# Two more row blocks transposed by DMA, and a new written-out order, in a four-layer attention kernel

## The chip, the core and the metric

The kernel runs on one core of a Trainium2 chip. The core has a matrix engine (TensorE, "PE" in the profile; its weight loads are shown apart as "PEld"), a vector engine (VectorE, "DVE"), an activation engine (ScalarE, "ACT"), a general engine (GpSimd, "POOL") and a queue engine that here only starts transfers (SyncE, "SP"). Each works through its own list of instructions in order; between lists there are only semaphores. The metric is the device time of one execution in microseconds (us). Three executions before the change took 422.68, 423.28 and 421.19 us; their median is 422.68.

## What is computed

The input is 2048 rows of 512 numbers. Four layers follow each other: linear attention (A), attention in a sliding window (B), A again and B again, the weights of A and of B being the same both times.

```python
def _A_ref(x, wqkv, wo):            # 32 heads of 16
    qkv = (x @ wqkv) ...
    phi = lambda t: jnp.where(t > 0, t + 1, jnp.exp(t)) + 1e-6
    pq, pk = phi(q), phi(k)
    kv = jnp.einsum("bhsd,bhse->bhde", pk, v)
    z = jnp.einsum("bhsd->bhd", pk)
    num = jnp.einsum("bhqd,bhde->bhqe", pq, kv)
    den = jnp.einsum("bhqd,bhd->bhq", pq, z)[..., None] + 1e-6
    return (num / den) ... @ wo

def _B_ref(x, wqkv, wo):            # 32 heads of 16, window of 256
    scores = jnp.einsum("bhqd,bhkd->bhqk", q, k) * (Dh ** -0.5)
    mask = (idx[:, None] - idx[None, :] >= 0) & (idx[:, None] - idx[None, :] < W)
    p = _softmax(jnp.where(mask, scores, -1e9))
    return jnp.einsum("bhqk,bhkd->bhqd", p, v) ... @ wo

x = x + _A_ref(_layernorm(x), A_wqkv, A_wo)
x = x + _B_ref(_layernorm(x), B_wqkv, B_wo)
x = x + _A_ref(_layernorm(x), A_wqkv, A_wo)
x = x + _B_ref(_layernorm(x), B_wqkv, B_wo)
```

A sum over all rows (`kv`, `z`) stands in the middle of each A layer: no row of it can be finished before the keys and values of every row are known. A B layer needs only the rows of its window.

## The kernel before

The rows are cut into 16 blocks of 128. All of x stays on the core (tiles `xres`, one for each block).

One block goes through a layer like this. DVE takes the statistics of its rows (lines 814, 815 and 817), POOL the inverse root (818), and DVE writes the normalised block `xn` (820). The matmuls need it transposed: `transp` (from line 823) does that either by a DMA transpose that SP starts (line 828), or by four PE transposes into PSUM (line 835) and a copy out of PSUM (line 845), which ACT or DVE can do. Which block goes which way is listed in `BYPE`. The transposed block is `xTa` in A layers, `xT` in B layers, and `oT` after attention, before the output projection.

PE then projects: keys, values and outputs with four 512-wide matmuls (line 858, two instructions of the plan for a projection), queries of A and queries and keys of B with sixteen 128-wide ones (line 870). In A layers, ACT and DVE compute phi (lines 879 to 885), PE adds keys times values up over the blocks (916), DVE masks the sum (1220), and PE and DVE make the outputs (942 to 954). In B layers, ACT or DVE copy the projections out of PSUM (keys at line 971, twice with a mask each; queries and values at 845), POOL starts DMAs that spread the values (981), PE makes scores (1007 for the two outer half pieces of the window, 1056 for the inner four pieces, 1063 for a mask in the last block), ACT takes their exponentials (1035, 1077), DVE masks them (1043, 1095), PE multiplies with the values (1113, 1125; 1158 and 1167 in the last block), DVE divides (1135, 1137), and the output projection is added to x (893 for A, 894 for B). The last block of the last layer is cut finer, so that the end is short (`b_end`, lines 1148 to 1213).

Keys and values of the third layer, with their sum in `kvacc` (1316), are interleaved with the attention of the second. So the run has these stages: keys and values of layer one; outputs of layer one and start of layer two; attention of layer two with keys and values of layer three behind it; the sum over all rows; outputs of layer three and start of layer four; attention of layer four; the end.

Nothing on the core decides the order. All the work is recorded as about 2,760 operations, and `ORDER` (line 328) is one long text that names them by number in the order in which they are to be laid out:

```python
for word in self.plan.split():
    word, _, at = word.partition(":")
    o = self.ops[int(word.rstrip("'"))]
    o.eng, cost = list(o.engs.items())[word.endswith("'")]
```

A number is an operation, the digits after a colon are the buffers or PSUM banks that its results take, and an apostrophe says that a copy goes to the second engine that can do it (DVE in place of ACT). Each engine's list is the sequence of its own operations in that text. Semaphore waits are then put in where an operation needs what another engine makes, or a buffer that another still uses. So the text sets the order on each engine, the split of the copies between ACT and DVE, and the use of the banks. The costs in the code (0.38 us for a group of transposes, and so on) only serve the laying out of such a text; the chip doesn't see them.

In the first layer, `BYPE` sends blocks one to six (numbers 0 to 5) through PE and the other ten through SP's DMA transposes. SP's list starts with the loads of x, between them one weight, and has the first layer's transposes next, the loads of the other weights (lines 775) behind them, and then the transposes of the later layers.

Of the kernel before, what the change touches and what calls it, by code (L numbers as in the profile page):

```python
# [334 lines left out]
230:5.0 194 299 231 184 224:4.0.0 200' 148 207:9 214:7.1 215 300 238:0 271:10 196 195 197 216 208:2.1.3 209 210 180 225 228 284 212 179 278:7.2 279 272:6.2.1  # L335
152 285 286:1 181 301 302:2 314 315 316 169 211 280' 255:11 226 227 229 273 317 213 318:3 256:3.3.2 257 274 239:12 232' 275 25 16 258 259 34 260 23 261 24
262:4.3 263 26 27 246:7.4 240:2.4.0 185 241 247 276 264' 287:13 244 288:5.5.3 201 289 303:14 290 291 310:6.5 311 312' 292 242 248 319:15 294:3.6 277 304:4.7.2
305 308 295 320:5.6.1 306 321 322 324 217 326:2.7 327 243 28 29 17 245 233 249 265 293 307 309 296' 281 297 313 323 328 325 329 330:0 331:1 378:7.4.0 379 380
# [9 lines left out]
658' 671 626 627 672 673 902:6 907:2 684 903 986:0.4.1 987 988 919 449:0 904 955 905:3 881:1 906:3 882:3 883 921:0.6.0 922 923 908 909 685 686:2 687:1 450:5  # L348
884 1407 960:3.0.3 451 961 910:2 911 677:2.1.5 678 912:2 989 962 1408 924 1409 452 474:6.0 475 476 488 477 478:2 479:3 937:3 938 679 933:0.4.1 934 935 674:2.1
675 700 701 1410 932 939 940:1 720 964:0.6.2 702 703 965 966 688:5.0 689 690 691 1411:3 936 942:4 1412:0 941:1 489:0.3 490 943 501 676' 1021:2.6.2 1022 944  # L350
1023 704:0 491 492 493:0 494:1 705:3 967 692:5.2 693 945:2 946 947:0 680 963 721 694' 956:0.2.0 957 958 954 480:4 481 482 644 645 662 1418:7.1 995:0.5.4 996
997 722:1 723:2 1419 1420' 990 913:4 914 915 968:0.2.5 969 970 495:7 496 713:6.2.0 714 715 959 503 497 504:0.0 505 999:4.2.1 1000 1001 972:7 971 977:6 506 973
507 508:3 1056:0.4.0 1057 1058 1024 736 737 974 975:1 738 976:2 978 979 991:0.2.0 992 980:3 981 1421 1422 1423 998 710:7.3 711 712' 993 706:6.1 707 708' 709'
1030:0.4.3 681 716 1031 1032 695:3.1.1 696 994 948:2 1002 1003:0.6.2 697' 1004 949 950 1435 509:3 982:2 510:5 983:4 984 1005 1006 663 1034:0.2.5 1035 985 1036
511 1012:7 512 772 1436 1437 739 1438 740:2 741:4 1060 1007:6 1008 1439:3 1440:2 1424 1449 1450 1091:0.4.1 1092 754 1093 513:3.12.1 514 515 1013 1014 1009
1010:2 1451 517 1011:0 1026:0.4.0 1027 1028 728:2.0 1015:0 1016 1413:3.1.0 1414 1415 729 755 1425:0 1426:1 698 1037 1065:0.6.1 1066 730' 1416 1417 1067
731:5.0.3 732 724:4.2 733 725 1038:0.2.2 1039 1040 1441:7.0.2 1446:6.0 1447 1442 1029 1025 1033 1042:5 1443 1069:0.2.4 1070 1071 726' 1095 1043 727'
1427:4.4.3 1428 1429 699 1452 1448' 1453:1 1041 1047:6 1044 1126:0.2.2 1127 756 1444 1445 1068 746:7.1 747 1017:1 1045:1 1454:5 1046:1 1128 1430 1431 1048
1094 1061:0.4.0 1062 1063 1049 748' 1050:3 1051 757 1052:0 758:2 759:0 1018:3 1019 1100:0.6.3 1101 1102 1020 1465 1466 1467 1460:2.4 773 774 1455:5.3.0 1456
1073:0.3.5 1103 1461 1074 1457 1462 1432:7.3 742:6.3 1433 743 1075 775 1072 1059 1064 1077:2 1078 744 1458 1459 1104:0.4.2 1105 1106 1076 1434' 1079 1082:3  # L360
1083 745' 1080:2 1081:3 516 717 1161:0.6.0 1162 1163 1084 1085:0 764:2.2 765 1086 518 1087:2 766' 1096:0.4.0 1097 1098 1130 749:3.1.2 750 767:2.2.4 776:3 1107
1165 1135:0.6.1 1136 751' 1137 768 769' 1053:5 777:3 1054 1108:0.3.4 1099 1055 1479 760:2.4 761 762' 1468 1109 1110 1111 734 1112:7 1139:0.5.5 1140 1141 1113
1114 763' 1115:1 770 1469:0 1117:4 1118 1116:2 752 1196:0.2.1 519:5.3 1129 520 1197 521 522 1198 523:0 524:3 1119 1120:2 543:7.13.2 544 545 1480 1121 547
1088:1 1199 1131:2.5.0 1142 1089 1090 782:4.3 783 1164 1493 1132 1133 1134 528:7.14.3 1138 1170:0.2.3 1171 784' 1172 529 530 532 778:6.5 779 780' 781' 525:5
526 1143:0.2.2 753 1144 1145 527 790 791 735 1147:4 1148 792 1122:1 1494 1149 1150:0 1146 1151:1 1174:0.6.4 1175 793 1176 794:1 546 1470:3 1476:5.2 1477
1471:3.2.0 1478' 1177 1472 1473 1474 1475 1152:4 1153 1231:0.6.2 1232 1233 1481 531 1482 1154 1155:1 1156 1123:5 533 1124 1166:0.2.0 1125 1507 1173 558:4.15.1
# [3 lines left out]
1484:4 1269 1504:4.6 1505 1204 812:0 1240:0.6.3 1241 1242 1158:2 1159 1502 1506' 1503 1510 1160 1523 1192:3 1524 1193:3 1194 1195 1537 807 1213:0.4.4 1214  # L370
813:2 1217:2 1215 1218 1219 1220:1 1221:2 1244:0.6.5 1245 1246 1485:3.7.1 549:4.3 1212 550 551 1538 552 553:3 554:1 1539 1216 1486 1487 1488 1489 818:2.1 819
820 814:1.1 1235 1236:4.6.0 1237 815 816' 1243 1238 821:0.2.0 822 823 1247 1239 1463:5.4 817 1275:2.6.1 1464 1222:0 1223 1224 1276 1277 1248:2.4.2 1249 1525
# [996 lines left out]
```

## Time and profile before

| | |
|---|---|
| median of 3 executions | 422.68 us (421.19 to 423.28) |
| the profiled execution | 422.47 us |
| its span, first to last instruction | 421.1 us |
| granted TensorE clock in the span | 1.000 |
| busy: PE, DVE, ACT, POOL | 392.3, 382.3, 383.6, 106.0 us |
| instructions of PE | 8330 matmuls, 8404 weight loads |
| DMA transposes | 115 (25 for xTa, 30 for xT, 60 for oT) |
| program loaded by queue q8 | 68 packets, 1.11 MB |

The profile is of one execution. "Busy" is the time in which an engine had at least one instruction in work, so overlapping instructions count once, while the duration of one instruction counts its whole way through the engine: two equal instructions that follow each other can start closer together than one takes. A matmul is two instructions, a weight load (PEld) and the matmul itself (PE). "Idle before" and "waited for" name who ended an idle time of an engine. "issue" stands where the profile shows no such cause. The chain of waits is found by going back from the last instruction, at each step to what released it.

### The profile page before, as it was taken

The page shows a single profiled execution, that of the slowest core. Times are in us where ns is not written, and L with a number is a line of the kernel's source. Part 1 is how long each engine was busy: PE and PEld are TensorE (multiplying, and loading weights), DVE is VectorE, ACT ScalarE, POOL GpSimd, SP SyncE. Part 2 cuts the span into 40 slices and gives each one's busy share as a digit, 9 for nine tenths or more (in the row PEclk, how much of TensorE's full clock was granted, in tenths as well). Part 3 has the DMA queues.
Part 4 walks back from the last instruction along what each step waited for, and adds up shares of the span by engine and source line. Part 5 has one row for each costly group of instructions (what it writes and reads, how often), then busy time and mean ns, then how long its engine had stood idle before and what let it go on. Part 6 is the DMA issues. An engine that isn't in the chain of part 4 may idle for free.

```text
span 421.1 us, 18887 instructions
## 1 busy us (share of the span) xinstructions
PE 392.3 (93%) x8330; PEld 284.2 (67%) x8404; DVE 382.3 (91%) x1003; ACT 383.6 (91%) x496; POOL 106.0 (25%) x202
## 2 busy tenths in 40 slices
PE   7999989999999899998999999998999899988997
PEld 3655766776766676767586667676767667666675
DVE  7999899999999899998999899999999999978774
ACT  4888679999999999999899767899999999999995
POOL 2230024225232231423131100332322212605200
PEclk9999999999999999999999999999999999999999
DMA  8334426314252130523141201324415422406143
GB/s 265 112 64 138 128 55 126 66 41 99 41 68 43 38 67 16 85 41 59 39 80 22 48 9 39 70 48 68 79 34 80 60 52 33 90 16 117 43 103 92
DMA packets 75720, 29.22 MB, mean 69 GB/s; under 512 B 65264, under 2 KB 73584, under 8 KB 75632
## 3 DMA queue, kind: packets, MB, share of 16 engines
q1 hardware_dynamic: 70336, 22.36, 26.4%
q0 software_dynamic: 4096, 4.46, 5.7%
q8 instruction: 68, 1.11, 1.1%
q10 hardware_dynamic: 1200, 1.11, 0.9%
q14 instruction: 20, 0.16, 0.1%
HBM read 6.29 MB, written 2.10 MB: 20 GB/s over the span
## 4 chain that ended last, share of the span: by engine, by line
PE 42%; ACT 33%; DVE 18%; issue 3%; DMA 3%; POOL 0%; DVEq 0%
ACT pF L1077 23%; PE ps L858 16%; PE ps L870 8%; ACT pH L1035 6%; PE ps L1125 6%; PE ps L1056 5%; PE ps L1113 3%; DVE stats L814 2%; DVE o L954 2%; ACT kbd L971 2%; DMA w_Av<-in_A_wqkv_dram 2%; DVE pF L1095 1%; DVE xres L893 1%; PE ps L916 1%; PE ps L1007 1%
## 5 line engine op out<-in xcount | busy, mean ns | idle before, releaser
L1077 ACT ACTIVATE pF<-ps 128x1024 bf16<-128x1024 f32 x240 | 229.4, 1085 | 4.4 <-PE ps L1056 2.6
L818 POOL TENSOR_TENSOR rstd<-mv,const 128x1 f32<-128x1 f32 x64 | 39.1, 617 | 241.6 <-DVE mv L817 238.6
L981 POOL DMA_DIRECT2D vbd<-vt x128 | 67.1, 532 | 48.2 <-DVE vt L845 30.6
L1035 ACT ACTIVATE pH<-ps 128x1024 bf16<-128x1024 f32 (+1 forms) x64 | 60.3, 1022 | 3.5 <-PE ps L1007 3.2
L1125 PE MATMUL ps<-vbd,pF 128*128 128x34 bf16 x1856 | 60.2, 178 | 2.4 <-issue 2.4
L1125 PEld LDWEIGHTS ps<-vbd,pF 128*128 128x128 bf16 x1856 | 53.3, 96 | 5.5 <-issue 2.7
L1056 PE MATMUL ps<-qT,kbd 32*128 32x128 bf16 x1920 | 48.5, 216 | 5.0 <-ACT pF L1077 2.1
L1095 DVE TENSOR_TENSOR pF<-pF,const 128x512 bf16<-128x512 bf16 (+2 forms) x116 | 46.6, 415 | 3.6 <-ACT pF L1077 3.5
L879 ACT ACTIVATE E<-ps 128x512 bf16<-128x512 f32 x64 | 40.1, 630 | 9.8 <-PE ps L870 6.4
L814 DVE BATCH_NORM_STATS2 stats<-xres 128x6 f32<-128x512 bf16 x64 | 44.0, 689 | 2.0 <-DMA xres<-in_A_x_dram 1.1
L1056 PEld LDWEIGHTS ps<-qT,kbd 32*128 32x128 bf16 x1920 | 28.5, 92 | 22.6 <-ACT pF L1077 9.6
L1043 DVE TENSOR_TENSOR pH<-pH,const 128x1024 bf16<-128x1024 bf16 (+1 forms) x64 | 41.1, 649 | 0.0
L870 PE MATMUL ps<-xT,w_Bq 128*128 128x128 bf16 x512 | 35.5, 219 | 1.0 <-ACT pF L1077 0.7
L870 PE MATMUL ps<-xT,w_Bk 128*128 128x128 bf16 x512 | 35.6, 219 | 0.6 <-ACT pF L1077 0.4
L1113 PEld LDWEIGHTS ps<-vbd,pH 128*128 128x128 bf16 x928 | 29.0, 96 | 8.3 <-issue 2.2
L870 PE MATMUL ps<-xTa,w_Aq 128*128 128x128 bf16 x512 | 34.2, 219 | 0.3 <-DVE pq L883 0.2
L858 PE MATMUL ps<-w_Ak,xTa 128*128 128x512 bf16 (+2 forms) x121 | 32.3, 372 | 1.6 <-issue 0.8
L858 PE MATMUL ps<-w_Av,xTa 128*128 128x512 bf16 (+1 forms) x128 | 32.7, 371 | 1.1 <-issue 0.5
L1113 PE MATMUL ps<-vbd,pH 128*128 128x34 bf16 x928 | 32.7, 178 | 0.9 <-DVE kbd L971 0.3
L858 PE MATMUL ps<-w_Ao,oT 128*128 128x512 bf16 (+2 forms) x119 | 29.4, 354 | 4.2 <-issue 1.6
L870 PEld LDWEIGHTS ps<-xT,w_Bk 128*128 128x128 bf16 x512 | 29.8, 98 | 5.0 <-issue 0.9
L870 PEld LDWEIGHTS ps<-xT,w_Bq 128*128 128x128 bf16 x512 | 29.5, 98 | 5.3 <-issue 2.0
(96 smaller groups left out, 625.6 us busy)
## 6 DMA issues: line engine op xcount, KB each, us to landing
vbd<-vt POOLq DMA_DIRECT2D x128, 34.0 KB, 2.4
xres<-in_A_x_dram SPq DMA_DIRECT2D x16, 128.0 KB, 5.7
out_dram<-xres SPq DMA_DIRECT2D x15, 128.0 KB, 2.3
oT<-o SPq DMA_TRANSPOSE x60, 2.8
w_Ak<-in_A_wqkv_dram ACTq DMA_DIRECT2D x1, 512.0 KB, 5.4
w_Av<-in_A_wqkv_dram ACTq DMA_DIRECT2D x1, 512.0 KB, 6.9
w_Aq<-in_A_wqkv_dram SPq DMA_DIRECT2D x1, 512.0 KB, 7.0
w_Ao<-in_A_wo_dram SPq DMA_DIRECT2D x1, 512.0 KB, 3.9
```

The lines of the kernel that those rows point to most:

```text
L814: s.op(n + ".st", {"DVE": 0.595}, lambda e, en: e.bn_stats(a_st, x.h[:]), reads=[x], writes=[st])
L858: i = e.matmul(g.h[:, a:b], xT.h[:, kt, :], w.h[:, kt, a:b], start=(kt == 0), stop=(kt == 3), skip_group_check=True)
L870: i = e.matmul(g.h[:, f * P:(f + 1) * P], w.h[:, kt, f * P:(f + 1) * P], xT.h[:, kt, :], start=(f == 0 and kt == 0), stop=(kt == 3), skip_ ...
L879: s.op(n + ".e", {"ACT": _act_cost(512)}, lambda e, en: e.activation(E.h[:], g.h, ACT.Exp, bias=0.0), reads=[g], writes=[E])
L981: return [e.dma_start(vbd.h[64 * a:64 * a + 64, j, a], vt.h[64 * j:64 * j + 64, a]) for j in range(2)]
L1035: return e.activation(d, c, ACT.Exp, bias=0.0, scale=DH ** -0.5)
L1043: return e.tensor_tensor(v, v, tr, ALU.mult)
L1056: i = e.matmul(ss[r // 2].h[:, r % 2, k * P:k * P + P], kbds[fj[m] // 2].h[32 * r:32 * r + 32, f, fj[m] % 2, :], qT.h[32 * r:32 * r + 32, ...
L1077: s.op("e%d%d" % (u, g), {"ACT": _act_cost(1024)}, lambda e, en, S=ss[g], pb=pb, g=g: e.activation(pb.h[:, 2 * g:2 * g + 2, :], S.h, ACT.E ...
L1095: return e.tensor_tensor(v, v, tr, ALU.mult)
L1113: i = e.matmul(U.h[:, c:c + 34], pH.h[:, 4 * r + f, 64 * a:64 * a + P], vbds[j // 2].h[:, j % 2, :, 4 * f + r, :], start=first[0], stop=Tr ...
L1125: i = e.matmul(U.h[:, c:c + 34], pFs[at[f, m][0]].h[:, r, at[f, m][1] * P:at[f, m][1] * P + P], vbds[fj[m] // 2].h[:, fj[m] % 2, :, 4 * f ...
```

## The change

`BYPE` is changed so that blocks five and six of the first layer (numbers 4 and 5) are no longer in it. Their transposes become DMA transposes that SP starts, and their two copies out of PSUM are no longer recorded, so there are two operations fewer and later numbers shift by two. The whole text of `ORDER` is replaced. The description of the change says that it was laid out with a late rule for instruction fetches. The rule itself is not in the code, only the order that came of it.

```diff
 ORDER = """
-37 4 0 3 6 7 1 8 9 2 68 61:7 69 70 5 67 71 72:0 73:6.0 62 38 66 85 86 87 10 39 40 88 41 42 43 44 45 46 11 33 12 13 20 47 89:1 22 74 75:7.0.0 76 90:6.1 81:5.0
...
+4 2 37 38 66 6 0 61:7 1 7 8 9 41 68 42 43 44 45 69 70 46 5 3 71 72:0 73:6.0 47 62 67 39 40 74 85 86 87 88 10 75:7.0.0 76 11 12 89:1 33 25 90:6.1 91 13 102
...
 """
-BYPE = {("x1.", t) for t in range(6)} | {("a2.", 15), ("k2.", 15), ("o3.", 0), ("x3.", 0), ("a3.", 15)} | {("o2.",0),("x2.",0)}
+BYPE = {("x1.", t) for t in range(4)} | {("a2.", 15), ("k2.", 15), ("o3.", 0), ("x3.", 0), ("a3.", 15)} | {("o2.",0),("x2.",0)}
```

What the new text does to the lists of the engines:

- PE: two groups of four transposes fewer. The rest are the same operations in another sequence, with the same stages block by block.
- SP: eleven loads of x in a row, then twelve transposes of the first layer, then the weights. Before, ten loads, two transposes, a load, and eight transposes stood there. The blocks' sequence was 6, 7, 9, 8, 12, 11, 10, 13, 14, 15 by number and is now 4, 5, 7, 6, 9, 8, 11, 13, 14, 10, 12, 15.
- ACT and DVE: of the copies that either can do, 24 full ones that DVE did go to ACT and 20 that ACT did go to DVE, and one small copy of the last block goes to ACT. Two copies of ACT, those behind the PE transposes, are gone.
- The end: the score matmuls of the last block's last piece stand ahead of, no longer behind, four matmuls of an output projection of another block and some of the last block's own matmuls with values.
- Buffers and PSUM banks are assigned anew throughout. The text ends a line earlier, so lines behind it have numbers that are lower by one in the new kernel.

More of the change, by code (lines that the diff above doesn't have):

```diff
@@ L348 @@
[L348 to L359, printed above, removed]
@@ new lines @@
+1019:0.6.2 1020 1021 501 944 690:3.2 691 987 478:2 954:0.4.0 955 956 692' 953 1022 479 678 1416:3.1 1417 716 993:0.6.4 1418' 911:5 912 965 994 995 480 913
+1419 966:0.3.5 703:3 967 711:2.2.0 502:6.1 945:1 660 661 957 503 504 505 493:5 494 495 968 969 712 713 997:0.3.1 998 999 506:2 970:5 975:2 971 1054:0.6.0 717
+718 719 734 735 972 976 977 1055 1056 752 753 989:0.3.0 679 990 973:2 974:3 978:3 979 1000 704:5.1 988 705 706' 707' 736 708:2.3 737 996 709 710' 714 991 992
+1028:0.6.3 1029 1030 1420 1421 720:1 507:3 508:4 1422 693:5.1.1 694 695' 1001:0.2.2 1002 1003 509 510 946:7 947 948 1032:0.5.5 1033 1005:4 1006 1004 1423:2
@@ new lines @@
+1134 1135 516 1085:1 1051:6 1097 1052 1053 765:7.2.4 1477 1106:0.4.2 1107 1108 766 767' 768 758:6.4 759 760' 761' 1137:0.2.5 1138 1139 775:3 1110:7 1111 1109
+517:4.2 518 519 520 1112 1113:3 1114:3 1115:6 521:0 1194:0.2.1 1195 1196 1086:7 1087 541:5.13.2 542 545 543 1116 1129:0.2.0 1130 1127 1131 1163 1088 750 751
+1136 1491 776:7.5 777 1128 778' 526:5.14.3 527 530 1117 779' 1168:0.2.3 522:2 780:7.3 1118:0 1119 1120:0 528 1132 529 531 781 782' 1478 1479 1480 523:6 524
+525 788 1492 789 790 1140 1169 1170 1141:0.4.1 1145:7 1142 1146 1143 1144 1147 1148:1 791 792:1 1149:1 1493 1172:0.2.2 1474:6.7 1469:5.7.0 1475 1173 1476'
@@ new lines @@
+793:1 1174 1175 1470 1471 1472 1150:4 769 1229:0.2.2 1230 1231 1121:7 1122 1473 1151 1494 1495:2 1496:4 1481:3 1482:7 1164:0.5.0 1123 1152 1505 1153:3 1154
+1171 1165 1166 1167 783:3.0.5 784 532:0.2 794:2.0 1155:3 533 534 535 536:2 1198 1506 1507 1203:4.6.4 785 801:3.1.1 802 803' 1204 1205 1206 795 796 797' 1180:5
+1176:0.6.5 1508 1181 1177 556:4.15.1 557 1178 558 1233 1179 1197 560 798:3.0 799 800' 1207:0.6.1 1208 1209 1182 1183:0 1184:0 1185:4 1186 1264:0.2.0 1265 1266
+1187 544 546 1188:1 1189 537:1 538:7 539 540 806 1199:0.5.0 1200 1201 807 808 1156:4 1157 1497:7.3.3 1158 1498 1499 1238:0.2.3 1239 1240 1690:6.16.0 1691
@@ new lines @@
+2326:0 2327:1 2318 2354 2347:0.4.2 1807:7 1808 1809 2025:6.2.4 2348 2349 65 2342 2374:0.2.1 2026 2322 2027' 2375 2298:7 2376 2299 2300 2066 2067 2387:0.4.5
+2328:6 1831:2.1 1832 1833 1834 2388 2389 2350 1835:3 1836:1 2068 2035:0 2028 2018:7.5 2019 2329 2330 2331:3 2020 2021 2390 2332 2346 2379:0.4.3 2380 2381 2377
+1822:3 2022:2.3 1823 2355:0.6.0 2356 1824 2084 2085 2023 2024' 2382 2359:5 2360 2357 2358 2383:0.3.4 2384 2361 2362:2 1837:2 1838 2229 2069 2070:1 2086 2385
+2363:2 2378 2029 1839 2102 2410:0.6.2 2411 2412 2262:5 2333:0 2036:4.0 2263 2264 2423:0.2.2 2424 2425 2037 2038 2386 1846:6.0 1847 1848 1849 2364:5 2087
@@ new lines @@
+2566 2590:5.0.1 2591 2592 2557 2541 2542:0 2115:3.2.4 2116 2337 2543:1 2547:1 2548 2571:4.6.4 2572 2573 2117' 2558 2126:2.5 2127 2128' 2129' 2595:0.4.5 2596
+2597 2574 2594 2570 2575:3 2576 2577 2578:3 2599:6.0.2 2579:0 2600 2478:2 2479 2480 2151:5.0.1 2626:3.6.2 2601 2627 2628 2513:1 2152 2153' 2602 2144:2.0 2145
+2598 2146' 2147' 2593 2606 2549:0 2639:0.3.0 2640 2580:5 2581 2582 2583:2 2584 2641 2642 2607:6.0.1 2608 2148:2.2 2149 2118 2119 2611:3 2631:6.4.4 2612 2150'
+2629 2442:2 2613 2614:0 2609 2615:3 2632 2610 2633 2161:1 2635:0.6.5 2636 2634 2637 2443 2444 2445 2514:5 2154 2155 2515 2516 2585:3 2662:0.3.0 2663 2664
```

87 lines of the change are left out of this document (33 added, 54 removed), and 82 rows, old and new, of the table ORDER.

## Prediction

> **What bounds the kernel now.** I began with the page.
>
> ```profile
> span 421.1 us, 18887 instructions
> PE 392.3 (93%) x8330; PEld 284.2 (67%) x8404; DVE 382.3 (91%) x1003; ACT 383.6 (91%) x496; POOL 106.0 (25%) x202
> PE 42%; ACT 33%; DVE 18%; issue 3%; DMA 3%; POOL 0%; DVEq 0%
> ```
>
> Three engines are busy nine tenths of the time and the chain of work that ended last passes through all three, so no single engine is the bound. The busy times were therefore read stage by stage (columns: stretch, its length, then the busy time of PE, PEld, DVE, ACT and POOL, clock, DMA share, GB/s).
>
> ```profile
> 0.00:44.60 44.60, 42.12 (x293) 23.09 (x298) 37.97 (x133) 34.09 (x60) 10.01 (x26) 1.00 0.53 158
> ...
> 110.00:160.00 50.00, 46.47 (x1099) 34.18 (x1100) 46.93 (x109) 47.49 (x58) 11.80 (x22) 1.00 0.28 47
> 160.00:200.00 40.00, 37.65 (x872) 27.70 (x882) 37.15 (x99) 39.12 (x49) 12.08 (x20) 1.00 0.32 53
> 200.00:252.00 52.00, 50.40 (x977) 35.91 (x985) 48.21 (x124) 44.05 (x61) 9.30 (x17) 1.00 0.22 40
> 252.00:281.00 29.00, 26.52 (x469) 20.41 (x472) 28.26 (x78) 24.84 (x40) 5.96 (x11) 1.00 0.28 54
> 281.00:405.00 124.00, 114.88 (x3008) 86.44 (x3029) 112.22 (x272) 122.87 (x139) 36.46 (x69) 1.00 0.36 62
> 405.00:421.10 16.10, 13.72 (x383) 10.18 (x385) 9.16 (x25) 11.42 (x16) 0.00 (x0) 1.00 0.38 94
> ```
>
> The first stage (keys and values of the first layer) belongs to PE: 42.12 of 44.60 us, most of the rest before its first weights land. From 160 to 200 ACT is idle for 0.88 us in 40, from 200 to 252 PE for 1.6 in 52, from 252 to 281 DVE for 0.7 in 29, and from 281 to 405 ACT for 1.1 in 124. An edit is worth something only on the engine that its stage belongs to.
>
> Next, what the chain of waits shows as time in which nothing visible was waited for, and PE's own list of waits.
>
> ```profile
> 117.92 0.60 issue
> 140.42 0.77 issue
> 151.20 0.68 issue
> 288.11 0.31 issue
> ```
>
> ```profile
> PE ps L1125 <- issue: 2.4, 4, 0.8
> ACT pF L1077 <- PE ps L1063: 0.7, 1, 0.7
> ```
>
> The four pieces are the first line of the waits: 2.4 us in four stops, each in the middle of a run of equal matmuls (probabilities times values, line 1125), where a wait for another engine makes no sense. Two stretches cut at the first three stops, and the DMA of the 2.4 us ahead of the second one, say what they are.
>
> ```profile
> 118.20:140.80 22.60, 21.14 (x500) 15.38 (x505) 21.29 (x54) 21.99 (x29) 6.52 (x13) 1.00 0.35 56
> 140.80:151.50 10.70, 9.77 (x252) 7.31 (x252) 9.64 (x22) 10.04 (x12) 4.07 (x8) 1.00 0.24 53
> ```
>
> ```profile
> q8 instruction: 1, 0.02, 3.7%
> ```
>
> Between stops lie 505 and 252 weight loads, each with its matmul: 1010 and 504 instructions, with the few semaphore instructions that are not counted 4 x 256 and 2 x 256. PE takes its program in pieces of 256 instructions, and each stop is such a piece arriving late. That is the "instruction fetch" of the change's title. The fetch does a second thing, which another piece of the chain and the DMA under it show:
>
> ```profile
> 56.26 4.38 DMA xT<-xn
> ```
>
> ```profile
> q8 instruction: 1, 0.02, 2.0%
> ```
>
> A DMA transpose with a fetch under way took 4.38 us; the transposes of the first stage usually took 2.5 (below). So the "late rule" can mean either: pieces of the program that come late, or transposes that land late beside a fetch. What the change says in code is only the new order.
>
> **Part 1: two row blocks to DMA.** Removed are two groups of four PE transposes and two copies by ACT (line 845).
>
> ```profile
> 18.13 0.39 PE L835 MATMUL ps<-const,xn 128*128 128x128 bf16 x4
> ```
>
> ```profile
> 16.30 0.86 PE ps L858 x4
> 17.16 0.89 PE ps L870 x16
> 18.06 0.24 PE ps L916 x4
> 18.30 0.22 PE ps L835 x4
> ```
>
> ```profile
> L845 ACT ACTIVATE xTa<-ps 128x512 bf16<-128x512 bf16 x7 | 4.5, 637 | 6.0 <-PE ps L835 5.9
> ```
>
> The timeline of PE (first row: start, length, line) gives block six's group 0.39 us, the chain (the next four rows: start, its share, line) 0.22, since it begins before the matmuls ahead of it end. I take 0.35, nearer the row that has the whole group: two groups give 0.7 us (0.4 to 0.8), and they count in full, since the stage is PE's. The two copies (1.3 us at 637 ns) leave an engine that is idle for 10.5 us of the stage: nothing.
>
> Added are two DMA transposes on SP's queue. Their cover:
>
> ```profile
> 14.00 0.40 DVE L820 TENSOR_SCALAR xn<-xres,mv,rstd 128x512 bf16<-128x512 bf16 x1
> ```
>
> ```profile
> 4.55 5.75 SPq L775 DMA_DIRECT2D xres<-in_A_x_dram  x10
> ...
> 21.08 16.17 SPq L828 DMA_TRANSPOSE xTa<-xn  x8
> ```
>
> ```profile
> DMA to landing us min/median/max: 2.4/2.5/2.5
> ```
>
> ```profile
> DMA to landing us min/median/max: 2.4/2.5/5.1
> ```
>
> (The two landing rows are those of tile xTa up to 45 us and over the whole run.) The normalised block five is ready at 14.4 in the old order; in the new one its place on DVE's list is earlier. SP has issued its loads by 10.3, and the eleventh, which now stands ahead too, adds some 0.6 us, so SP waits for DVE and not the other way. Landing takes 2.5 us, or 5.1 at worst, so the block is there between 16.9 and 19.5. When PE needs it follows from the chain rows: at 16.30 in the old order PE had done all that the new one puts ahead of block five's first key matmul, but for one key and one value projection (0.86 each), one query projection (0.89) and one 0.24, while block five's transpose (0.35) falls away: 16.30 + 2.85 - 0.35 = 18.8. The block is covered by 1.9 us, or costs 0.7 at worst; I take nothing. Block six is needed two projections and a 0.24 later, and I take its cover to be the same. Behind the transposes in SP's queue stand the weights of the later stages. Eight issues with their waits took 16.17 us; twelve from 14.4 would, even at that rate, end at 38.7 instead of 37.3, and the stage that uses these weights begins after 44.6. Nothing moves there.
>
> **Part 2: the new order.** Every engine's list is rearranged, but block by block the sequence of stages is the same. Three differences can be priced.
>
> The stops. From start to start of the rows below come the paces: 0.34 us for 16 scores of line 1056, 0.41 for 16 of lines 1125 and 1113, 0.35 for 32 of line 1007; the chain rows above give 0.22 for one of line 858 and 0.89 for 16 of line 870. With these I added up the PE work in each piece of 256 instructions:
>
> ```profile
> 138.24 0.40 PE L1056 MATMUL ps<-qT,kbd 32*128 32x128 bf16 x16
> 138.58 0.57 PE L1125 MATMUL ps<-vbd,pF 128*128 128x34 bf16 x16
> 138.99 0.56 PE L1113 MATMUL ps<-vbd,pH 128*128 128x34 bf16 x16
> ...
> 139.88 0.41 PE L1007 MATMUL ps<-qT,kbd 32*128 32x64 bf16 x32
> 140.23 0.19 PE L1125 MATMUL ps<-vbd,pF 128*128 128x34 bf16 x1
> ```
>
> The pieces ahead of the stops at 117.92, 140.42 and 151.20 hold 3.6, 2.7 and 2.9 us of work in the old order; in the new order the pieces at the same three counts hold 4.8, 4.2 and 4.2, and the shortest piece anywhere holds 3.3 instead of 2.7. Short pieces are consumed before the next has come, so I expect these three stops to go. The piece ahead of 288.11 holds 4.7 us in the old order and 4.9 in the new: there shortness was not the cause, and its 0.3 may stay. The worth of all this lies between nothing (ACT, idle 2.5 us from 110 to 160, would be the next late one, or pieces of 3.3 stop in their place) and 2.4 us. I take 1.4, two thirds of the first three stops' 2.05, nearer the upper end because the chain runs through each of them.
>
> The Trainium skill, Runtime: NRT & Kernel Launch, section "Instruction fetch mechanics", speaks against this gain: the sequencer fetches the next block of 256 instructions while it executes the current one, and the cost of crossing a boundary is mostly hidden. The trace agrees on the 256 and not on the cost, with its 2.4 us in four stops. By the page the gain of 1.4 would be nothing.
>
> The end. In the old order ACT's last two exponentials waited 0.7 us for the score matmuls (the second waits row above), and ahead of these stood, among others, an output projection of another block:
>
> ```profile
> 411.90 1.30 PE ps L858 x6
> ```
>
> In the new order four of these six, and three groups of values matmuls, stand elsewhere: the scores come over 0.86 us earlier. The ACT wait of 0.7 bounds the gain above; nothing is the lower bound, as the values matmuls now follow later. I take 0.6.
>
> The copies out of PSUM. By the lists, 24 full copies went from DVE to ACT and 20 the other way: four more for ACT, beside one small one at the end. Counted by place on ACT's list: four more between the scores of blocks twelve and sixteen of layer two (about 163 to 226 us), one fewer up to the next layer's scores, one more net behind them.
>
> ```profile
> 95.67 1.15 ACT kbd L971 x2
> ...
> 269.98 1.32 DVE kbd L971 x2
> ```
>
> One costs ACT 0.575 and saves DVE 0.66. Three fall where ACT has 8 us of idle time in 52: covered, and 1.7 us if that cover is gone. One falls where ACT has 0.88 in 40, one in the stage that belongs to ACT: 1.15 us at most, nothing at least. I take 0.8, a loss. What DVE saves, 2.6 us, comes ahead of the stage of 252 to 281 that is DVE's, in one that is PE's: I take nothing, and 2.6 as the bound.
>
> Sum: -0.7 - 1.4 - 0.6 + 0.8 = -1.9. The profiled execution took 422.47 us with 1.4 around its span; 422.47 - 1.9 = **420.6**. The median of the three runs, 422.68, is 0.2 above the profiled one. What I can't read from lists is whether 2,760 rearranged operations bring small waits of their own.
>
> **The rivals.** *The fetch costs nothing.* ACT, at 47.49 of 50 us, is late next when PE's stops go, or other pieces stop. For it speaks ACT's share, against it that the chain stays on PE through all three stops. Time: 422.47 - 0.7 - 0.6 + 0.8 = 422.0. This is also how it would go by the page's sentence.
>
> *The copies hit ACT.* If the new order closes the idle time that ACT has from 200 to 252, all four copies delay the exponentials behind them, 2.3 us. It decides once less than 2.3 of those 8 us is left on ACT, and then PE's stops and the end gain nothing, as ACT would have been late anyway: 422.47 - 0.7 + 2.3 = 424.1, slower than before. For it speaks that ACT is full on both sides of the stage; against it that PE, with 1.6 us idle in 52, is what ACT waits for there.
>
> *DVE's relief arrives.* If the shorter DVE list lets the third layer start early, its 2.6 us come on top: 418.0. Against it: PE had no room ahead of that barrier.
>
> **How the numbers follow.** Forecast 0.44, fetch costs nothing 0.27, copies hit ACT 0.18, DVE's relief 0.11. About 0.5%, 2.1 us, is what a measurement of this kernel can tell from no change, so "faster" begins at 420.6: half of the forecast, the last rival and a little of the rest, 0.40. "Slower" begins at 424.8, beyond the second rival's own time; a third of that rival with new waits added, and a tenth of what is left, give 0.15. The rest, 0.45, is no change. The forecast's own range, from its bounds, is -0.7 - 2.4 - 0.7 = 418.7 to 422.5; with the other cases 417.8 to 424.2.
>
> **What would show it.** After: no "issue" wait at line 1125, or one under 0.8 us in total; line 835 on xn with 28 matmuls and the first stage's last key-value matmul some 0.7 us before 44.6; no wait of PE for xTa's DMA at 19 to 22 us; no ACT wait for line 1063 at the end; ACT busy about 1 us longer and DVE 2 to 3 us shorter. Wrong would be: stops of the same total elsewhere, PE waiting for a transpose in the first 25 us, or an ACT that is idle more than 37.5 us in all.

## The result, and the profile after

| | before | after |
|---|---|---|
| median, the two kernels run in turn | 421.75 us (421.06 to 423.28) | 419.05 us (418.38 to 419.54) |
| ratio, 95% interval | 1 | 0.9929 [0.9913, 0.9944] |
| the profiled execution | 422.47 us | 418.38 us |
| its span | 421.1 us | 417.1 us |

The change makes the kernel 0.7% faster: 2.7 us by these medians, 3.0 by the ratio of 0.9929; the prediction was 1.9 us. The two profiles lie 4.1 us apart because that of before is 0.7 us above its median and that of after is the fastest of six. Of any difference between these two traces some 1.4 us is therefore the choice of the execution.

The head of the page after, with the busy times, the chain's shares by engine, and a group that had stops before (its last two columns: mean ns of one, idle time ahead of it):

```profile
span 417.1 us, 18964 instructions
PE 401.3 (96%) x8402; PEld 283.5 (68%) x8402; DVE 379.2 (91%) x998; ACT 383.3 (92%) x499; POOL 106.7 (26%) x202
ACT 47%; PE 41%; DVE 10%; issue 1%; DVEq 0%
L1124 PE MATMUL ps<-vbd,pF 128*128 128x34 bf16 x1856 | 59.6, 178 | 0.0
```

Lines of code behind the text are one lower than before, so line 1124 is the old 1125. The 2.4 us that it waited for nothing visible are zero. "Issue" has gone from 3% to 1% of the chain, some 8 us, but the stops are only 2.4 of them. PE's busy time can't be compared as it stands, since the trace of before has 74 matmul records fewer than weight loads, all of them at line 858; that of after lacks none. Where such a record is missing the profile shows PE idle, mostly for 0.16 us, although it worked, and about 3.5 us of the fall of "issue" stand at this line. ACT is as busy as before (383.3 for 383.6 us), DVE 3.1 us less. Line 834 on xn now has 28 matmuls for 36, and no wait of PE for an xTa made by DMA is in the list of the first 45 us.

The stages after, cut at the same events as before where a stage got shorter (stretch, length, busy PE, PEld, DVE, ACT, POOL):

```profile
0.00:43.55 43.55, 41.89 (x289) 22.44 (x290) 38.30 (x135) 31.73 (x58) 10.94 (x26) 1.00 0.58 169
...
110.00:160.00 50.00, 48.85 (x1136) 34.84 (x1138) 47.73 (x119) 48.59 (x60) 16.04 (x30) 1.00 0.28 51
160.00:200.00 40.00, 39.57 (x877) 28.28 (x877) 36.97 (x96) 39.63 (x52) 8.25 (x16) 1.00 0.34 58
200.00:249.10 49.10, 48.48 (x955) 34.36 (x953) 43.68 (x115) 42.72 (x60) 9.72 (x17) 1.00 0.19 37
```

From 110 to 249 us PE is now idle for 2.2 us in 139.1; the same stretches of before had 7.5 in 142. Most of this fall is not the chip's. The same two stretches for line 858 alone (line 857 after; busy PE, PEld) show it:

```profile
110.00:252.00 142.00, 53.78 (x231) 21.41 (x258) 1.00 0.27 46
```

```profile
110.00:249.10 139.10, 58.22 (x258) 21.36 (x256) 1.00 0.26 48
```

For as many weight loads before has 27 matmul records fewer and 4.4 us less busy time. PE's real idle time before was therefore some 3.1 us, 2.05 of them the three stops. The first stage is a microsecond shorter.

Where the time went is read best from the start of the same operation in each trace. "Stage one" is the first masked sum of layer one (line 1220, DVE); "block 12" the first exponential of block 12 in layer two; "sum" the first masked sum of layer three; "block 16" the first exponential of the last block in layer four; "last" the last operation of DVE (line 1213). All in us, from the traces.

| trace | stage one | block 12 | sum | block 16 | last | span |
|---|---|---|---|---|---|---|
| before | 44.60 | 163.57 | 252.19 | 403.90 | 419.54 | 421.1 |
| after | 43.55 | 160.46 | 249.11 | 400.07 | 415.31 | 417.1 |
| difference | -1.05 | -3.11 | -3.08 | -3.83 | -4.23 | -4.0 |

So 1.05 us come from the first stage, 2.06 from the stretch that held three of the four stops, nothing from there to the sum (the stretch of the copies), 0.75 from there to block 16 of layer four, and 0.4 from the end. These are two executions. With nothing changed in it, the first stage ends between 44.25 and 44.60 us in three traces of the old order, and at 43.55 and 43.80 in two of the new one.

The 0.75 us are not the fourth stop, which lay in that stretch: two traces of the old order without it (experiment 1 with +66, and experiment 2) took 151.8 us for the stretch, before took 151.7, and after took 151.0. ACT, which the prediction gave this stage to, has less to do there (busy PE, PEld, DVE, ACT, POOL; before, then after):

```profile
252.19:403.90 151.71, 140.43 (x3453) 106.11 (x3480) 139.56 (x344) 146.42 (x176) 42.42 (x80) 1.00 0.35 61
```

```profile
249.11:400.07 150.96, 144.38 (x3480) 106.20 (x3478) 138.97 (x344) 145.43 (x175) 43.19 (x80) 1.00 0.35 62
```

No run takes this part of the new order alone.

### The profile page after: what moved, and what is told of

Read it like the earlier page. It is cut to its first block, busy times and chain, and to the rows that moved or that the text cites. A ratio compares the mean times of both kernels' runs of the same rounds, so it can differ in the third digit from the quotient of the medians.

```text
span 417.1 us, 18964 instructions
## 1 busy us (share of the span) xinstructions
PE 401.3 (96%) x8402; PEld 283.5 (68%) x8402; DVE 379.2 (91%) x998; ACT 383.3 (92%) x499; POOL 106.7 (26%) x202
## 4 chain that ended last, share of the span: by engine, by line
ACT 47%; PE 41%; DVE 10%; issue 1%; DVEq 0%
ACT pF L1076 33%; PE ps L857 17%; ACT pH L1034 9%; PE ps L869 8%; PE ps L1055 4%; PE ps L1124 4%; PE ps L1112 2%; PE ps L915 2%; ACT kbd L970 2%; DVE o L953 1%; DVE xres L892 1%; DVE stats L813 1%; ACT E L878 1%; PE ps L1253 1%; ACT vt L844 1%
## 5 line engine op out<-in xcount | busy, mean ns | idle before, releaser
L857 PE MATMUL ps<-w_Bv,xT 128*128 128x512 bf16 (+2 forms) x152 | 35.7, 346 | 0.3 <-ACT vt L844 0.2
L857 PE MATMUL ps<-w_Ao,oT 128*128 128x512 bf16 (+2 forms) x144 | 34.5, 356 | 0.7 <-ACT pF L1076 0.6
L857 PE MATMUL ps<-w_Ak,xTa 128*128 128x512 bf16 (+1 forms) x134 | 33.6, 369 | 0.6 <-ACT xTa L844 0.5
L857 PE MATMUL ps<-w_Bo,oT 128*128 128x512 bf16 (+2 forms) x140 | 33.0, 355 | 0.7 <-ACT pF L1076 0.6
L857 PE MATMUL ps<-w_Av,xTa 128*128 128x512 bf16 (+2 forms) x133 | 33.6, 371 | 0.0
```

Source lines behind the costliest of these rows:

```text
L857: i = e.matmul(g.h[:, a:b], xT.h[:, kt, :], w.h[:, kt, a:b], start=(kt == 0), stop=(kt == 3), skip_group_check=True)
```

## The experiments

Each was timed against the kernel before in the same session; the median of before moved between 421.8 and 422.6 us from session to session, so ratios are compared. In the tables the trace of each kernel is set against the trace of the one that it was made from.

### 1. Other cuts of TensorE's program, by a longer warm-up

Three kernels change nothing but the number of warm-up matmuls ahead of the branch into the main part. Every later instruction of PE then stands at another place in its 256-instruction piece.

```diff
-        s.op("warm", {"PE": 4.5}, warm(11), ...)
+        s.op("warm", {"PE": 4.5}, warm(44, 128), ...)
+        s.op("warm", {"PE": 4.5}, warm(59, 95), ...)
+        s.op("warm", {"PE": 4.5}, warm(99, 57), ...)
```

Old order, 44 matmuls of 128 columns:

> The kernel before with one edit: the 11 warm-up matmuls of 512 columns become 44 of 128, so that every later PE instruction stands 66 places further on in the 256-instruction pieces of PE's program; order, engines and waits are the same. Theory S (the gain in the middle of the run is the four stops of PE for a piece of its program, and a stop comes where a piece holds too little work): the shortest pieces hold 3.1, 3.4 and 3.6 us instead of 2.7, 2.8 and 2.9, so the stops fall from 2.4 us to under 0.9 and the time falls by 1.0 to 1.5 us (ratio 0.997). Rival O (ACT covers the stops, the gain is that of the order's own waits): stops gone or not, time within 0.4 us of before.

New order, 59 of 95 columns:

> The changed kernel with 59 warm-up matmuls of 95 columns for 11 of 512: its program stands 96 places further on in the pieces; the shortest piece then holds 3.45 us. Theory S: no stops, time within 0.5 us of the changed kernel (about 419, ratio 0.993). Rival L (the new order is fitted to where each fetch meets a DMA transpose, and gains by that): other transposes land late now, PE or ACT waits for them, and the time is 1 us or more above the changed kernel's.

New order, 99 of 57 columns:

> The changed kernel with 99 warm-up matmuls of 57 columns: 176 places further on, where the shortest pieces hold 2.8, 3.1 and 3.3 us. Theory S: stops come back, 0.6 to 1.8 us in all, and the time is 0.4 to 1.5 us above the changed kernel's. Rival O: at most 0.3 us above it, whatever the stops. Rival L: as for the shift by 96, 1 us or more above with and without stops.

All three were slower: 1.0146 [1.0123, 1.0169], 1.0108 [1.0085, 1.0130] and 1.0117 [1.0083, 1.0151] of the kernel before. Read by the total they would have refuted the stops. The offsets against their own base say where it came from:

| trace | stage one | block 12 | sum | block 16 | last |
|---|---|---|---|---|---|
| old order, +66 | +5.94 | +4.91 | +4.93 | +5.04 | +5.03 |
| new order, +96 | +7.15 | +7.30 | +7.19 | +6.94 | +8.12 |
| new order, +176 | +8.20 | +8.41 | +8.74 | +9.42 | +10.19 |

The greater part of the loss, 5.9 to 8.2 us, is in the first stage, where the granted clock was 0.50 from 10 to 15 us (the last section shows it). Behind it, each kernel tells what it was made for. In the old order the longer pieces gain 0.9 us from stage one to the last operation, with one stop of 0.8 us left, at line 1007; a further 1.2 us are lost behind the last operation, as in experiment 2. In the new order long pieces cost nothing until 401 us, and then one stop of 1.0 us brings 1.2; short pieces lose 2.0 us in pieces of 0.2 to 0.8. PE's waits in the latter (engine, line, what it waited for; total, times, longest; from 200 us on):

```profile
PE ps L1124 <- issue: 1.0, 4, 0.5
...
PE ps L1112 <- issue: 0.7, 2, 0.4
```

and the one stop of the former:

```profile
PE ps L1062 <- issue: 1.0, 1, 1.0
```

Same matmuls, same neighbours, other cuts: stops come, go and move, and cost the end about what they last. The +96 row also speaks against a reading in which the new order wins by fitting transposes around program fetches: all fetches moved there, and 350 us of the run kept their offset within 0.4 us.

### 2. The same in the old order, without spoiling the start

```diff
-        w2 = s.op("warm2", {"PE": 0.6}, warm(2, 384), ...)
+        w2 = s.op("warm2", {"PE": 0.6}, warm(35, 16), ...)
```

> Old order, with 33 tiny warm-up matmuls more (66 instructions, 16 columns each in place of two of 384) behind the branch, where TensorE waits for the first weight anyway, so that its later 256-instruction pieces begin elsewhere and the shortest is 3.1 us of work, not 2.7. If the stops of TensorE were the late pieces and are worth about 1.0 us (what the run with the longer warm-up ahead of the branch left, once its spoilt start is taken off): the stops at 118, 140, 151 and 288 us are gone, the start is within 0.2 us of the kernel before, and the time is 0.9975 of it (421.1 for 422.15). If other engines take up what the stops leave: the start is the same, the later stages are too, and the ratio is 1.000.

Measured: 422.80 us, 1.0017 [1.0002, 1.0031]: no gain. Its trace has both a gain and a loss. PE's waits:

```profile
PE ps L1007 <- issue: 0.8, 1, 0.8
...
PE ps L1125 <- issue: 0.3, 1, 0.3
```

1.1 us of stops stand where 2.4 stood, and the last DVE operation comes at 418.57 instead of 419.54. The span is 421.3 nevertheless, 0.2 longer. The transfers out at the end (timeline: start, us of issuing, queue, line, count) in this kernel, with the operation that makes the last one's data, then in the kernel before:

```profile
417.08 2.47 SPq L896 DMA_DIRECT2D out_dram<-xres  x2
...
417.87 0.42 DVE L1205 TENSOR_SCALAR xres<-ps 128x256 bf16<-128x256 f32 x1 [0.22 <-PE ps L1195]
...
419.59 0.43 SPq L1209 DMA_DIRECT2D out_dram<-xres  x1
```

```profile
418.04 0.93 SPq L896 DMA_DIRECT2D out_dram<-xres  x2
419.28 0.33 SPq L1209 DMA_DIRECT2D out_dram<-xres  x1
```

Its two issues at 417 us took 2.47 us, not 0.93, and the last one started 1.3 us after its data were there (417.87 + 0.42). In just that time the DMA shows a program fetch, which the extra 66 instructions brought into the end of the run (queue, packets, MB, share; 417 to 419.3 us):

```profile
q8 instruction: 1, 0.02, 4.4%
```

The fetch was not isolated by a run of its own, but the traces of all 14 kernels of this text agree: of SP's 224 transfers out, 51 were issued with a program fetch under way, and 30 of these took 0.77 to 2.02 us to issue; of the 173 others none took more than 0.59.

How large the stops are in an ordinary execution of the old order is told by the four further runs below that keep its cuts: line 1125 stopped for 3.0, 1.0, 1.8 and 2.2 us there, 2.4 in the profile of before, 2.1 on the mean. These runs also show what a stop is worth, since none of them changes the work between stage one and block 12. The stops in that stretch and its length, in all seven traces of the old order:

| trace | stops, us | stage one to block 12, us |
|---|---|---|
| experiment 3, first try | 2.25 | 119.28 |
| before | 2.05 | 118.97 |
| experiment 7, copies to ACT | 1.57 | 118.40 |
| experiment 6 | 1.23 | 118.41 |
| experiment 1, +66 | 0.83 | 117.94 |
| experiment 2 | 0.83 | 117.95 |
| experiment 3, second try | 0.82 | 117.86 |

A microsecond of stops makes the stretch about 0.9 us longer, and the line through the seven points gives 117.2 us without any (an estimate). The three traces of the new order that have no stop there took 116.9 to 117.1 us. So nearly all that the new order gains in this stretch is the stops.

### 3. The two transposes alone, in the old order

```diff
-BYPE = {("x1.", t) for t in range(6)} | ...
+BYPE = {("x1.", t) for t in range(4)} | ...
 ORDER: 141:6.4 becomes 141:4, 158:7.5 becomes 157:5, the copies 142 and 159 fall away
```

First with a changed warm-up ahead of the branch (19 matmuls of 296 columns) to keep the cuts:

> The kernel before with part 1 alone: blocks five and six of the first layer are transposed by DMA at the place in the old order where their PE transposes stood, and 19 warm-up matmuls of 296 columns replace 11 of 512, so that the 16 PE instructions that fall away don't move the pieces of PE's program. Step 1 of the prediction: the first stage ends 0.7 us earlier (0.4 to 0.8) and the time falls by 0.7. Rival T (the transposes land too late): PE waits for xTa between 15 and 22 us, gain 0 to 0.4. Rival H (hidden later): the stage ends 0.7 earlier, the time falls by less than 0.3 because ACT or DVE is late next.

422.59 us, 1.0011 [0.9996, 1.0027]; but the trace was 0.65 us late at stage one, and a late start from the warm-up could not be told from a loss by the part. So again with the filler behind the branch:

```diff
-        w2 = s.op("warm2", {"PE": 0.6}, warm(2, 384), ...)
+        w2 = s.op("warm2", {"PE": 0.6}, warm(10, 77), ...)
```

> Old order, only blocks five and six of the first layer transposed by DMA; eight small warm-up matmuls behind the branch stand in for the 16 instructions that fall away, so that TensorE's pieces begin where they did. The first try of this had a changed warm-up ahead of the branch and a start 0.6 us late, ahead of any effect of the part. If the two groups are worth their work on TensorE: the first stage ends 0.7 us sooner and the time is 0.998 of the kernel before (421.4 for 422.15). If the transposes land too late in the old order, or the stage is not TensorE's: the first stage ends when it did or later, TensorE waits for a DMA-made xTa between 15 and 22 us, and the ratio is 1.000 or above. The stops stay in both cases.

422.21 us, 1.0012 [0.9998, 1.0027]: no gain, and the first stage ends 0.12 us later. Waits of PE and of its weight loads in the first 45 us of this kernel, then of before:

```profile
PEld ps L857 <- DVE pk L882: 1.0, 3, 0.6
...
PE ps L915 <- ACT xTa L844: 0.4, 1, 0.4
```

```profile
PEld ps L858 <- DVE pk L883: 0.4, 2, 0.2
...
PE ps L916 <- ACT xTa L845: 0.2, 1, 0.2
```

PE has 0.7 us less to do and waits for it elsewhere. The time of the first group becomes a longer wait for ACT just behind it, at 16.0 us. Behind the second group PE runs 0.27 us ahead of before (a value matmul starts at 19.54 for 19.81 us), and at 24.8 us it is level again, because the next key matmul waits until DVE is done with a buffer (line 882), and DVE is no sooner than before. At 29 us it waits for DVE once more and is 0.11 us behind. From 20 to 25 us PE, ACT and DVE were busy for 5.00, 5.00 and 4.92 of 5 us in before, so this part of the stage was not PE's alone. No wait is for a DMA-made xTa, so the transposes are in time. (The 0.7 us that this trace is ahead of before at the end go with its smaller stops, 1.0 us for 2.4.)

### 4. The two transposes undone, in the new order

```diff
-BYPE = {("x1.", t) for t in range(4)} | ...
+BYPE = {("x1.", t) for t in range(6)} | ...
 ORDER (numbers with the two copies counted): 336 141:6.4 142 ... 145 158:5.5 159
```

> New order, with blocks five and six of the first layer transposed by TensorE again, their two copies on ACT, in banks that are free there; the rest of the text is the new one. If moving the transposes is worth TensorE's work of two groups: the first stage ends 0.7 us later than in the new kernel and the time is 0.9945 of the kernel before (the new kernel has 0.9929). If that part is worth nothing and the whole gain is the text's: 0.993, and the first stage ends as in the new kernel. Pieces of TensorE's program are at least 3.4 us of work here, so no stops are expected in either case.

421.82 us, 0.9997 [0.9983, 1.0010], and stage one 2.65 us later: far more than the transposes. PE's waits:

```profile
PE ps L834 <- ACT pq L881: 1.7, 1, 1.7
...
PE ps L857 <- ACT xTa L844: 0.9, 2, 0.5
```

The first group waited 1.7 us for bank 6, which ACT was still reading. That prices the bank that I chose, not the part. With other banks and places:

```diff
 ORDER: 111 141:7.4 142 ... 145 158:6.5 159
```

> New order, blocks five and six of the first layer transposed by TensorE as before the change, each group in a bank that its last reader has left by the trace of the new kernel (the first try waited 1.7 us for a bank that ACT still read). If moving the two transposes is worth what TensorE spends on them: the first stage ends 0.7 to 1.0 us later than in the new kernel (43.6 us) and the time is 0.9945 to 0.9955 of the kernel before (the new kernel has 0.9929). If the sooner end of the first stage comes from the new text alone: the stage ends as in the new kernel and the ratio stays 0.993. More than 1.5 us later: the copies out of PSUM on ACT, which is full from 10 to 20 us, cost more than the transposes.

419.41 us, 0.9929 [0.9907, 0.9950]. The interval holds both expectations. The trace is sharper:

| trace against after | stage one | block 12 | sum | block 16 | last | span |
|---|---|---|---|---|---|---|
| banks 6 and 5 | +2.65 | +2.80 | +2.78 | +2.61 | +2.82 | +2.8 |
| banks 7 and 6 | +0.79 | +1.00 | +0.95 | +0.72 | +0.83 | +0.8 |

0.8 us appear in stage one and stay to the end. That is one pair of traces, and not only PE's work: PE waits for the copy of a transposed block for 1.0 us in this one and for 0.5 in after. Of the further 0.2 at block 12 a stop of TensorE near 72 us is the likely cause, as the 16 instructions move the cuts:

```profile
PE ps L1055 <- issue: 0.5, 1, 0.5
```

### 5. One block more by DMA

```diff
-BYPE = {("x1.", t) for t in range(4)} | ...
+BYPE = {("x1.", t) for t in range(3)} | ...
 ORDER: 124:4.3 becomes 124:3, the copy 125 falls away; warm2 as warm(10, 77)
```

> New order, and block four of the first layer transposed by DMA too, its PSUM copy left out; eight small warm-up matmuls behind the branch keep the pieces of TensorE's program where they are. If a block moved to DMA is worth 0.35 to 0.5 us as long as it lands in time: the first stage ends that much sooner, 0.992 of the kernel before. If its transpose lands too late, since block four's keys are needed some 3 us after it is normalised and SP still issues loads: TensorE waits for it near 16 us, and the time is that of the new kernel (0.993) or up to 1.5 us above it (0.9965).

420.07 us, 0.9938 [0.9915, 0.9961]; stage one ends 1.5 us later than after. PE's waits up to 45 us:

```profile
PE ps L856 <- DMA xTa<-xn: 1.9, 1, 1.9
```

Block four is needed too soon for this way. It is the wait that the prediction feared for block five, one block earlier.

### 6. The end alone, in the old order

```diff
 ORDER: 2661 64 2588:5 2589 2695:2 2722 ... 2591 2714:2.1 2716 2715:6 2730:4
     becomes 2661 2714:4.1 2716 2715:6 64 2588:5 2589 2695:2 2722 ... 2591 2730:4
```

> Old order, with one thing of the new one: the score matmuls of the last block's last piece, its exponential and its mask matmul stand ahead of the output projection of block 14 and the last block's own value matmuls. If the end is worth what the prediction gave it: ACT's wait for the mask matmul is gone, everything up to 405 us is as before, and the end comes 0.6 us sooner (0.9986; bounds 0 to 0.7). If the wait only moves to the next engine in the chain of the end: 1.000.

The scores also take another bank here, 4 for 2. 423.22 us, 1.0034 [1.0020, 1.0047]: slower. ACT's wait for the mask matmul is gone and the last exponential starts 0.56 us sooner than in before, but the last DVE operation comes 1.73 us later, 1.5 of it behind block 16. The waits from 405 us on:

```profile
PE ps L857 <- ACT pF L1076: 1.2, 1, 1.2
```

The output projection that now stands behind waits for a bank that ACT's exponentials leave later, since one more stands ahead of them. The wait moved from ACT to PE, as the second theory had it, and grew.

### 7. Four copies, from both sides

The same four copies are given back to DVE in the new order, and to ACT in the old one. An apostrophe sends a copy to DVE.

```diff
 new ORDER: 839 1548 1562 814       become  839' 1548' 1562' 814'
 old ORDER: 841' 1550' 1564' 816'   become  841 1550 1564 816
```

> New order, but four of the copies that went from DVE to ACT (values of block 15 of layer two, values of blocks 10 and 11 of layer three, half the keys of block 14 of layer two; about 190 to 235 us) are done by DVE again. If the four more copies cost ACT 0.8 us, as the prediction has it: the time is 0.8 us lower, 0.991 of the kernel before. If ACT's idle time covers them: the time stays at 0.993. If DVE has no room for them there: above 0.994, by up to 2.6 us (0.999).

422.25 us, 0.9995 [0.9980, 1.0009]: nearly the whole gain of the change is gone. In the trace 2.4 of its 3.6 us arise between block 12 and the sum (+0.94 and +3.32 against after); two stops, of 0.6 us near 73 us and 0.3 near 409, are most of the rest. PE's waits between block 12 and the sum, in this kernel; in the trace of after the only wait for a copy in that list is one of 0.2 us:

```profile
PE ps L915 <- DVE vA L844: 1.2, 1, 1.2
PE ps L1112 <- ACT kbd L970: 0.3, 1, 0.3
```

> Old order with nothing changed but four copies moved from DVE to ACT, the same four that cost 3.2 us when they were given back to DVE in the new order (values of block 15 and half the keys of block 14 of layer two, values of blocks 10 and 11 of layer three). If more copies on ACT cost time, as the prediction's term has it: 0.8 us more, 1.002 of the kernel before. If what they free on DVE was the price of the stage from 190 to 252 us: that stage is up to 2.2 us shorter (what the new kernel gained there) and the ratio is 0.995. If either split only fits the order that it was laid out with: 1.000 or above, up to 1.006. TensorE's list is untouched, so its stops stay as they are.

423.46 us, 1.0020 [1.0006, 1.0034]: slower as well, by 0.8 us by the ratio. From block 12 to the sum the trace goes from -0.75 to +0.89, 1.6 us, of which one stop is 0.3. What waits there is DVE, for ACT's exponentials of phi (this kernel from 185 to 255 us, then before to 253):

```profile
DVE E L879 <- ACT E L878: 2.5, 2, 2.3
```

```profile
DVE E L880 <- ACT E L879: 0.4, 1, 0.4
```

## Why the prediction was right, and where it was not

The forecast of "a little faster, by the stops, the first stage and the end" came true in direction and nearly in size. By its steps:

- **The first stage, -0.7.** Right in size for the new order: in one pair of traces undoing the part costs 0.8 us there and keeps it to the end. The times of those two kernels don't tell them apart (0.9929 both). The working was incomplete. It said that the work counts in full because the stage is PE's; in the old order the same part brought nothing, because ACT and DVE were as full as PE where the time came free, and PE only waited more for them. The share of busy time was not enough to say so; what is next in PE's list had to be free too.
- **The stops, -1.4.** Right, in mechanism and in size. The stops follow the cuts of PE's program (experiment 1), and a microsecond of them is worth 0.9 (experiment 2). From stage one to block 12 they took 1.6 us on the mean of five executions with the old cuts, against the 1.4 of the forecast; the 2.06 us of the profiled pair are the worth of one execution's three stops (2.05). None is left at that line after, but the new order is not free of stops in every execution: with the same PE program, experiment 7 had two, of 0.6 and 0.3 us. The Trainium skill, Runtime: NRT & Kernel Launch, section "Instruction fetch mechanics", has the cost of such a crossing mostly hidden. The trace of after agrees, with its 68 packets of program and no stop at line 1124; in that of before, with as many packets, four crossings cost 2.4 us.
- **The fourth stop,** of which the prediction said that it may stay, since its piece was not short, went too, and was worth nothing: without it the stretch to block 16 took as long. It went with the longer warm-up alone as well, so the cuts decide it, and the length of one piece is not the whole rule. The 0.8 us stop at line 1007 in both shifted old orders, and the one of 1.0 us in the new order with long pieces, say the same. Why a piece of 4.7 us of work ends in a stop stays open.
- **The end, -0.6.** The sign named for it is there: no ACT wait for the mask matmul. Behind block 16 the trace of after is 0.4 us shorter. But the mechanism alone, in the old order, lost 1.5 us from block 16 to the last operation. The gain belongs to the whole arrangement of banks and matmuls at the end; that the earlier scores bring it is not shown.
- **The copies, +0.8.** This is the step that failed. The prediction took a count of copies per engine, priced it with the idle times of the old order and added it to a sum for the new order. In the new order the stretch from block 12 to the sum took the same time as before (88.65 for 88.62 us), and four copies placed the old way cost 2.8 us (0.9995 less 0.9929, of 421.8; 2.4 in that stretch of the trace). In the old order four copies to ACT did cost 0.8 us by the ratio, but that the number fits is luck: the trace lost more, between block 12 and the sum, where the prediction had counted on ACT's 8 us of idle time to cover the copies. ACT's busy time was to grow by about 1 us and fell by 0.3, and in the stage of layer four that belongs to ACT, where a copy more was to cost up to 0.6, it fell by 1.0.
- **Not in the sum:** 0.75 us from the sum to block 16 of layer four. The prediction had only the fourth stop and one copy more there. So it is luck too that the sum without the copies, -2.7 us, is what the medians show: the end gave less than its term, and this stretch gave what had no term.

The range of the forecast, 418.7 to 422.5, is not what its bounds add up to: with the least gains (0.4, nothing, nothing) and the dearest copies (1.15) the upper end is 423.2.

Of the rivals, "the fetch costs nothing" falls by the table of experiment 2. "The copies hit ACT" resembles what the old order does, where DVE then waits for ACT, and the new one does not. "DVE's relief arrives" gave DVE 3.1 us less work, yet the sum came not a moment sooner relative to block 12, so the relief did not add to the gain; that it is needed to hold the stage where it was is what experiment 7 suggests.

## What to carry to other kernels

A laid-out order is one piece: the two transposes, the earlier scores and the four copies gained nothing or lost when put into the old order one by one, and the same four copies cost 2.8 us when taken out of the new one. So price an edit by the waits around it in the order in which it will run, not by the idle time of the order that it leaves. When an engine stops in the middle of equal instructions, shift its program by a few dozen instructions and see whether the stop moves, and read such a test by offsets between milestones, not by the total, since the filler has a price of its own. And compare the number of matmul records with that of weight loads before reading idle time: 74 missing records made PE look idle where it was not.

## What was not expected of the hardware

**A longer program ahead of the branch.** Thirty-three matmuls more ahead of PE's branch, with as many columns in all, cost 5.9 us at the start. Windows of 5 us of that kernel (the last three numbers are the granted clock, the DMA share and GB/s):

```profile
0.00:5.00 5.00, 3.81 (x36) 3.81 (x37) 2.22 (x9) 2.58 (x2) 1.33 (x11) 1.00 0.51 144
5.00:10.00 5.00, 0.97 (x10) 0.80 (x8) 4.09 (x17) 0.00 (x0) 1.59 (x3) 0.92 1.09 377
10.00:15.00 5.00, 4.83 (x18) 2.15 (x19) 0.14 (x1) 1.85 (x4) 0.06 (x1) 0.50 0.56 193
15.00:20.00 5.00, 4.95 (x36) 2.73 (x36) 4.89 (x19) 2.57 (x6) 1.24 (x3) 0.90 0.02 3
```

PE is busy for 0.97 us from 5 to 10 us, and then runs at a granted clock of 0.50. In before, the first two program fetches that the trace shows on queue q8 start at 2.30 and 8.56 us and the clock stays at 1.00; here they start at 7.58 and 12.15 us. The +96 kernel shows the same (0.50 from 10 to 15 us). The order of events, a late fetch, an idle PE and then a halved clock, is what the traces show; which one causes which was not tried.

**Fetches and other transfers.** In the trace of before, transposes with a program fetch under way landed after 3.4 us (median of 71), the others after 2.5 (44); in that of after, after 3.3 (74) and 2.4 (43). The new order did not avoid the encounters, and this lateness is not what changed. What may have changed is who waits for it: behind the first stage PE waits over 0.15 us for a late transpose in four of the seven traces of the old order, for 0.2 to 1.4 us in all, and in one of the seven of the new order, for 0.6. In two of the four (experiment 6, and the first try of experiment 3) this was a wait for an xTa at 200 us, of 0.9 and 0.6 us, and the stretch from block 12 to the sum took 89.4 and 89.0 us where four others took 88.6 to 88.7. That issuing a transfer out can take 1.5 us longer beside a fetch is shown in experiment 2.
